# A three-layer kernel on one core: one written order for every loop step, the K split by DMA, and a fixed order where the second expert layer starts

## The chip, the cores and the metric

One core of one Trainium2 chip runs the whole program. The metric is the device time of an execution in microseconds (us). PE is TensorE, DVE is VectorE, ACT is ScalarE, POOL is GpSimd, SP is SyncE, which here only issues DMAs (its queue is SPq). Each engine works through its own queue in order; between engines the order is kept by semaphores.

## The reference

Three layers follow one another; the output is that of the third. All matrices are float32.

```
scores = (q @ k.T) / 8                        # 4 batches, 8 heads, 576 x 576, head size 64
kth    = 32nd largest score of the row
attn   = softmax(scores where scores >= kth)
x      = attn @ v                             # as 2304 tokens x 512
h      = x @ w_in                             # 512 x 2048
y      = (h * clip(h + 3, 0, 6) / 6) @ w_out  # 2048 x 512
logits = normed(y) @ normed(expert_emb).T / tau     # 8 experts
e, gate = argmax(logits), softmax(logits)[e]
out    = gate * (relu(y @ w1[e]) @ w2[e])     # 512 x 1024, 1024 x 512; each token by its own expert
```

## The kernel before, in words

Every float32 product is made of three faster ones: an operand is rounded to a high part (a cast on ACT), the low part is the difference (a subtraction on POOL or DVE), and high x high, high x low and low x high add up in PSUM.

**The loop.** The attention is cut into 72 units (128 rows of two heads, or a remainder of 64 rows of four). `step(i)` runs 76 times and issues, in one fixed order, pieces of five units in different stages: the scores of unit i (PE L368, copied by ACT L371, paired maxima on DVE L380 to L384), the 32 largest values of unit i-1 (`select`, DVE L399 and L402), the masking of unit i-2 (`relu` on ACT L416, `mask` on POOL L420), the exponent of unit i-3 (ACT L426) with its sum, reciprocal and scaling (POOL L430, DVE L433, POOL L442; ACT L440 for the first 16 units), and the transposes (PE L453, copies ACT L458) and the product with v (PE L471) of unit i-4. `manual_schedule` means that each engine's queue has the instructions in the order in which the program issues them.

**The second layer inside the loop.** Two 128-token groups that are done are pushed as eight items; from step 12 on each step takes one item (none in the steps named in `PAUSE`): `s1` (24 matmuls, PE L530), `gate`, `swish`, `large`, `small`, and, for the item of the step before, `s2` (2 x 6 matmuls, PE L563). The low parts of the weights come back from DRAM (`fetch`, 512 KB each, SP L251).

**The weights of the second layer** arrive as 64 pieces of 64-bit words. `convert_w` takes two pieces at a time: it first calls `load_w`, which issues loads as long as fewer than five pieces are waiting (buffers `stg`, five), then makes float32 of the words on DVE (L221, L223, L229), ACT (L226) and POOL (L227); `split_w` makes the high part (ACT L240), the low part (POOL L241) and stores that (SP L236). One pair per step in steps 0 to 7, then two.

**K.** `load_k` loads each head twice, into partitions 0 to 63 and 64 to 127, in two halves of 288 columns (SP L288, buffers `kraw`, five). `need_k` casts all (ACT L296) and the upper 64 partitions get the low part by a subtraction, one half on POOL (L349), the other on DVE (L352).

**Routing.** A finished group y goes through four side steps, one per loop step: `r1` (squares, transposes), `r2` (logits, DVE maximum and index, one-hot L609), `r4` (rank among the tokens of its expert by a triangular matmul, L615, L616, and the running count `acc` on POOL), `r5` (table row, DVE L626, L627, and a scatter into the table `tbl` by POOL L628).

**After the loop** no order is written; the tile scheduler sets it. The remaining items run back to back (`whole`). Once 16 groups are counted (`order`), `ahead` starts the third layer: the first expert's weights, the ids of its first 256 tokens, its gathers, the split of w1. After the last items the last two groups are routed; only then are all ids known. `stage1` is the first product of an expert (PE L917), `stage2` the second (PE L930), `split2` the split of w2 (ACT L734, DVE L735), `tokens` gathers tokens (POOL L750) and transposes them (PE L754), `load_ids` reads the table (SP L716).

Of the kernel before, what the change touches and what calls it, by code (L numbers as in the profile page):

```python
# [8 lines left out]
F32 = mybir.dt.float32  # L9
# [29 lines left out]
PAUSE = (13, 17, 31, 35, 49, 53, 66, 67)  # L39
HS = S // 2  # L40
# [4 lines left out]
SIDE = 100  # L45
# [38 lines left out]
def layers(tc: tile.TileContext, qt, kt, v, w_in, w_out, embt, tau, w1, w2, out, y_dram, g_dram, x_dram, tbl, lo_dram, flag, pools, consts):  # L84
# [13 lines left out]
    acc = const.tile([128, E], BF16, name="acc")  # L98
# [3 lines left out]
    viol = const.tile([128, NUNIT, 2, 2], BF16, name="viol")  # L102

# [32 lines left out]
    def embed(part):  # L136
# [6 lines left out]
        elif part == 1:  # L143
            onesf = mp.tile([128, 128], F32, tag="ug", name="onesf", bufs=4)
# [15 lines left out]
    def setup():  # L160
        nc.vector.memset(ones, 1.0)
        nc.vector.memset(acc, 0.0)
        nc.gpsimd.iota(iota8, pattern=[[1, 8]], base=0, channel_multiplier=0, allow_small_or_imprecise_dtypes=True)
        nc.gpsimd.iota(ebase, pattern=[[STRIDE, 8]], base=0, channel_multiplier=0, allow_small_or_imprecise_dtypes=True)
# [5 lines left out]
        padt = mp.tile([128, E * STRIDE * 2 // 128], I32, tag="ug", name="padt", bufs=4)  # L170
        nc.gpsimd.memset(padt, PAD)
        nc.sync.dma_start(out=tbl.rearrange("(p a) b -> p (a b)", p=128), in_=padt)
        zr = mp.tile([128, DM], F32, tag="ug", name="zr", bufs=4)
# [7 lines left out]
    wpieces = deque()  # L181
# [7 lines left out]
    wraw = deque()  # L189
    whole_w, small_w = deque(), deque()  # L190
    cnt = [0]

    def load_w():

        while wpieces and len(wraw) < 5:
            src, dst = wpieces.popleft()
            if src.dtype == F32:
# [5 lines left out]
            wraw.append((raw, dst, src.dtype == F32))  # L203

    def convert_w():


        load_w()
        words, two = [], [wraw.popleft() for _ in range(min(2, len(wraw)))]
        if not two:  # L210
            return
        both = mp.tile([128, DM], F32, tag="ug", name="wf", bufs=4)
        for o, (raw, dst, single) in enumerate(two):
            full = both[:, 256 * o:256 * o + 256]
            if single:
                nc.vector.tensor_copy(full, raw)
            else:
                cnt[0] += 1
                words.append((raw, full.bitcast(I32), cnt[0] % 4 != 3))
        for raw, t, _ in words:  # L220
            nc.vector.scalar_tensor_tensor(t, raw[:, :, 1], 3, raw[:, :, 1], op0=ALU.logical_shift_left, op1=ALU.bitwise_xor)  # L221
        for raw, t, _ in words:
            nc.vector.scalar_tensor_tensor(t, t, 0x3FFFFFFF, raw[:, :, 1], op0=ALU.bitwise_and, op1=ALU.bitwise_xor)  # L223
        for raw, t, rounded in words:
            if rounded:
                nc.scalar.activation(raw[:, :, 0], raw[:, :, 0].bitcast(U32), AF.Copy, scale=2.0 ** -29)  # L226
                nc.gpsimd.tensor_tensor(t, t, raw[:, :, 0], op=ALU.add)  # L227
            else:
                nc.vector.scalar_tensor_tensor(t, raw[:, :, 0], 29, t, op0=ALU.logical_shift_right, op1=ALU.bitwise_or)  # L229
        whole_w.append((both,) + two[0][1])  # L230

    def split_w():

        while small_w:
            lo, full = small_w.popleft()
            nc.sync.dma_start(out=lo, in_=full)  # L236
        while whole_w:
            full, hi, lo = whole_w.popleft()
            x = full if len(hi.shape) == 2 else full.rearrange("p (k n) -> p k n", k=2)
            nc.scalar.copy(hi, x)  # L240
            nc.gpsimd.tensor_tensor(x.bitcast(F32R), x, hi.bitcast(F32), op=ALU.subtract)  # L241
            small_w.append((lo, full))
# [4 lines left out]
    def fetch(n, m):  # L247

        if m < total and m not in lows_[n]:
            lows_[n][m] = t = lop.tile([128, 1024], F32R, tag=f"l{n}", name=f"lo{n}")  # L250
# [25 lines left out]
    low, low2 = deque(), deque()  # L276
# [3 lines left out]
    def load_k(i):  # L280
# [3 lines left out]
        for h in (2 * p, 2 * p + 1):  # L284
            if (b, h) not in K and (b, h) not in kraws:
# [4 lines left out]
    def need_k(b, h):  # L290
        if (b, h) in K:
            return
        t = kp.tile([128, S], F32R, tag="k", name="kst")
        for g, raw in enumerate(kraws.pop((b, h))):
            c = slice(HS * g, HS * g + HS)
            nc.scalar.copy(t[:, c], raw)  # L296
            (low if g else low2).append((t[64:128, c], raw[64:128, :], t[64:128, c].bitcast(F32)))
        K[b, h] = t
# [27 lines left out]
    def prep(i):  # L326
# [15 lines left out]
        if u[0] == "t":  # L342
            need_k(u[1], 2 * u[3])
            need_k(u[1], 2 * u[3] + 1)

    def lows():
# [3 lines left out]
        while low2:  # L350
            o, x, h = low2.popleft()
            nc.vector.tensor_tensor(o, x, h, op=ALU.subtract)  # L352
# [737 lines left out]
```

## Time and profile before

| | |
|---|---|
| time, median of 3 runs | 1183.14 us (1183.0 to 1194.14) |
| the profiled execution's own time | 1184.85 us |
| its span, first to last instruction | 1183.1 us |
| PE busy | 1026.0 us (87%), 7224 matmuls |
| DVE busy | 838.1 us (71%) |
| ACT busy | 732.1 us (62%) |
| POOL busy | 645.7 us (55%) |
| mean granted TensorE clock | 0.938 of 2.4 GHz |

An engine's busy time is that of its instructions, without its waits. The granted clock is given as a share of full speed: 1.00 is 2.4 GHz, 0.50 is 1.2 GHz, and a value between them is a stretch that had both. Matmuls overlap, so their single durations add up to more than the time they take.

### The profile page before, as it was taken

The page shows a single profiled execution, that of the slowest core. Times are in us where ns is not written, and L with a number is a line of the kernel's source. Part 1 is how long each engine was busy: PE and PEld are TensorE (multiplying, and loading weights), DVE is VectorE, ACT ScalarE, POOL GpSimd, SP SyncE. Part 2 cuts the span into 40 slices and gives each one's busy share as a digit, 9 for nine tenths or more (in the row PEclk, how much of TensorE's full clock was granted, in tenths as well). Part 3 has the DMA queues.
Part 4 walks back from the last instruction along what each step waited for, and adds up shares of the span by engine and source line. Part 5 has one row for each costly group of instructions (what it writes and reads, how often), then busy time and mean ns, then how long its engine had stood idle before and what let it go on. Part 6 is the DMA issues. An engine that isn't in the chain of part 4 may idle for free. (4 is left out here: it accounts for less than half of the span.)

```text
span 1183.1 us, 21477 instructions
## 1 busy us (share of the span) xinstructions
PE 1026.0 (87%) x7224; PEld 885.8 (75%) x7224; DVE 838.1 (71%) x2714; ACT 732.1 (62%) x1518; POOL 645.7 (55%) x846
## 2 busy tenths in 40 slices
PE   2476766699999899999899999999998898999994
PEld 1354555578888788888788878889987787888883
DVE  6999977998899998899998899611244343445440
ACT  5688768777777877777877787642334343444540
POOL 5667767686777786777786766623231433113200
PEclk9966778789999999999999998999998899999997
DMA  7335555655324445424454333346781564244540
GB/s 212 120 100 174 164 177 187 195 179 197 122 90 155 127 160 184 121 89 155 115 183 157 121 92 115 110 142 178 210 276 32 187 217 171 71 176 147 174 166 20
DMA packets 97113, 176.49 MB, mean 149 GB/s; under 512 B 21135, under 2 KB 46882, under 8 KB 96991
## 3 DMA queue, kind: packets, MB, share of 16 engines
q1 hardware_dynamic: 92351, 164.90, 43.4%
q0 software_dynamic: 4640, 10.10, 2.5%
q8 instruction: 60, 0.98, 0.3%
q14 instruction: 62, 0.51, 0.1%
HBM read 155.87 MB, written 19.71 MB: 148 GB/s over the span
## 5 line engine op out<-in xcount | busy, mean ns | idle before, releaser
L420 POOL TENSOR_TENSOR s<-s,z 128x576 f32<-128x576 f32 x144 | 186.0, 1292 | 13.0 <-ACT z L416 11.5
L530 PE MATMUL bank_h<-xh,vh 128*128 128x256 f32 x576 | 172.1, 299 | 2.7 <-ACT xh L488 1.6
L530 PE MATMUL bank_h<-xh,lo 128*128 128x256 f32 x576 | 166.7, 289 | 7.1 <-DMA lo<-lo_dram 7.1
L530 PE MATMUL bank_h<-xl,vh 128*128 128x256 f32 x576 | 166.2, 288 | 0.6 <-DVE xl L489 0.6
L399 DVE MAX8 A<-left 128x8 f32<-128x288 f32 (+1 forms) x288 | 160.0, 596 | 0.0
L453 PE MATMUL bank_t<-ident,s 128*128 128x128 f32 x648 | 110.2, 297 | 53.1 <-ACT s L440 26.1
L547 POOL TENSOR_TENSOR gl<-u,gh 128x512 fp32r<-128x512 f32 x72 | 93.2, 1294 | 79.0 <-ACT gh L544 78.0
L453 PEld LDWEIGHTS bank_t<-ident,s 128*128 128x128 f32 x648 | 76.1, 149 | 75.8 <-ACT pt L458 37.7
L368 PE MATMUL ps_sc<-kst,qh 128*128 128x288 f32 x256 | 88.8, 359 | 49.1 <-ACT s L371 24.1
L536 ACT ACTIVATE u<-bank_h,half 128x512 f32<-128x512 f32 x72 | 49.5, 687 | 118.9 <-PE bank_h L530 118.9
L563 PE MATMUL y<-wh,gh 128*128 128x512 f32 x288 | 120.0, 418 | 0.0
L530 PEld LDWEIGHTS bank_h<-xh,vh 128*128 128x128 f32 x576 | 113.3, 197 | 8.1 <-issue 3.1
L530 PEld LDWEIGHTS bank_h<-xh,lo 128*128 128x128 f32 x576 | 113.2, 196 | 8.3 <-DMA lo<-lo_dram 8.3
L563 PE MATMUL y<-lo,gh 128*128 128x512 f32 x288 | 115.9, 403 | 0.0
L530 PEld LDWEIGHTS bank_h<-xl,vh 128*128 128x128 f32 x576 | 113.4, 197 | 1.4 <-DVE xl L489 1.0
L735 DVE TENSOR_TENSOR l<-a,h 128x1024 fp32r<-128x1024 f32 x64 | 77.4, 1232 | 51.9 <-ACT h L734 45.7
L563 PE MATMUL y<-wh,gl 128*128 128x512 f32 x288 | 114.2, 401 | 0.0
L416 ACT ACTIVATE z<-s,zb 128x576 bf16<-128x576 f32 x144 | 112.7, 782 | 1.0 <-DVE zb L405 0.8
L426 ACT ACTIVATE s<-s,nb 128x576 f32<-128x576 f32 x144 | 111.7, 775 | 0.0
L458 ACT COPY pt<-bank_t 128x384 f32<-128x384 f32 x216 | 95.6, 479 | 24.4 <-PE bank_t L453 24.4
L540 DVE SCALAR_TENSOR_TENSOR u<-u,bank_h 128x512 f32<-128x512 f32 x72 | 49.2, 684 | 83.8 <-ACT u L536 83.7
L471 PE MATMUL bank_a<-pt,vt 128*64 128x128 f32 (+1 forms) x1600 | 105.4, 285 | 0.0
(230 smaller groups left out, 2819.9 us busy)
## 6 DMA issues: line engine op xcount, KB each, us to landing
lo<-lo_dram SPq DMA_DIRECT2D x144, 512.0 KB, 4.3
a<-in_moe_w_dram SPq DMA_DIRECT2D x64, 512.0 KB, 8.7
kraw<-in_k_dram SPq DMA_DIRECT2D x64, 144.0 KB, 2.6
qraw<-in_q_dram SPq DMA_DIRECT2D x64, 128.0 KB, 3.3
w<-in_moe_w_in_dram SPq DMA_DIRECT2D x32, 256.0 KB, 3.9
w<-in_moe_w_out_dram SPq DMA_DIRECT2D x32, 256.0 KB, 3.5
lo_dram<-wf SPq DMA_DIRECT2D x32, 256.0 KB, 2.1
vt<-in_v_dram SPq DMA_DIRECT2D x16, 320.0 KB, 4.1
```

The lines of the kernel that those rows point to most:

```text
L368: nc.tensor.matmul(ps[:, n, :HS], t, kk[:, HS * g:HS * g + HS], start=(o == 0), stop=(o == len(parts) - 1))
L399: nc.vector.max(A[:, n, 8 * r:8 * r + 8], src[:, n, :w])
L416: nc.scalar.activation(zb_[n], tile_of(i, n), AF.Relu, bias=sel[i][2][:, n:n + 1], scale=-BIG)
L420: nc.gpsimd.tensor_tensor(s, s, zb_[n], op=ALU.subtract)
L426: nc.scalar.activation(s, s, AF.Exp, bias=sel[i][1][:, n:n + 1], scale=SCALE, accum_out=sums[i][:, n:n + 1])
L453: nc.tensor.transpose(pp[:, 128 * k:128 * k + 128], e[:, 128 * (3 * c + k):128 * (3 * c + k) + 128], ident)
L458: nc.scalar.copy(pts[i][:, 3 * c:3 * c + 3, :].rearrange("p k n -> p (k n)"), tb_.pop((i, c))[:, :384])
L471: nc.tensor.matmul(av[64 * n:64 * n + 64, c0:c1], vt[:, k, 64 * n:64 * n + 64], pt[:, k + 5 * n if k < 4 else 4, c0:c1], start=(o == 0), s ...
L530: nc.tensor.matmul(ph[:, a, :], w, x[:, k, :], start=(k == 0 and n == 0), stop=(k == 3 and n == 2))
L547: nc.gpsimd.tensor_tensor(state[q][1], state.pop((q, "u")).rearrange("p (a n) -> p a n", a=2), state[q][0].bitcast(F32), op=ALU.subtract)
L563: nc.tensor.matmul(state["y"][o], x[:, a, c], w, start=(f == 0 and n == 0), stop=(f == 15 and n == 2))
L735: nc.vector.tensor_tensor(lo, x, hi.bitcast(F32), op=ALU.subtract)
```

## The change

**The loop step** becomes a table of names: `FIRST` for steps 0 to 20, `THEN` for the others. Each name is one piece of work as before; a few are cut finer (`s1` into its two halves, the weight conversion into `load`, `one`, `two`, `round`, `add`, `hi`, `low`, `store`). Weights are loaded one step ahead of their conversion (`load` has offset -1), one pair per step in steps 0 to 4 and two from step 5 on, and split and stored one step after it.

**K** is loaded once, two heads in one tile of 128 partitions; ACT casts it into both heads' tiles, POOL subtracts in place over all 128 partitions, and two DMAs (`ship`) carry the low halves into the other 64 partitions. DVE has no part in it.

**The threshold** of the mask (DVE L405, two per unit) moves into the POOL instruction that scales the maximum (`bounds`).

**Routing** of groups 0 to 11 is done four groups at a time: `choose` (one-hot picks and running counts), `rank` (table rows), and `place`, one scatter per step.

**The last two groups** are routed in a written order together with the first products of the first expert (two of their eight blocks, `stage1(0, 0, 256, (o,))`, stand between the transposes) and with the split of its second weights; the second expert's first weights (`load1(1)`) are loaded ahead of all that. The side steps after the loop get priority 600 instead of 100.

```diff
+RAMP, WORDS = 5, 21
+FIRST = ("turn0 lows ship hi0 expo0 low0 hi1 s10 keep0 load_k expo1 turn1 bend0 one0 guard pick0 store0 score0 low1 two0 mask0 pick1 "
+         "turn2 inverse s11 pick2 round1 bend1 keep1 take0 keep2 load_q mask1 s20 score1 round0 gate one1 scale two1 values swish "
+         "take1 large aside add0 store1 pick3 pairs load0 add1 xh load1 s21 small bounds xl prep need_v")
+THEN = ("pick0 turn0 turn1 expo0 keep0 s10 expo1 lows ship turn2 pick1 pick2 s11 keep1 keep2 guard bend0 score0 gate take0 load_k "
+        "values mask0 score1 inverse swish scale pick3 bend1 xh load_q take1 prep need_v mask1 bounds aside large s20 xl pairs "
+        "s21 small place")
...
-SIDE = 100
+SIDE = 600
...
+    def pair_of(i, c):
+        n = (i if c == 0 else -1) if i < RAMP else 2 * i - RAMP + c
+        return n if 0 <= n < 32 else -1
...
-                kraws[b, h] = [lp.tile([128, HS], F32, tag="kraw", name="kraw", bufs=5) for _ in range(2)]
-                for g in range(2):
-                    nc.sync.dma_start(out=kraws[b, h][g], in_=kt[b * H + h][:, HS * g:HS * g + HS])
+            kraws[b, p] = raw = lp.tile([128, S], F32, tag="kraw", name="kraw", bufs=2)
+            for n in range(2):
+                nc.sync.dma_start(out=raw[64 * n:64 * n + 64, :], in_=kt[b * H + 2 * p + n][64 * n:64 * n + 64, :])
...
+        nc.scalar.copy(k0, raw)
+        nc.scalar.copy(k1, raw)
+        low.append((raw.bitcast(F32R), raw, k0.bitcast(F32)))
+        ships.append((k0[64:128, :].bitcast(F32), raw[0:64, :]))
+        ships.append((k1[0:64, :].bitcast(F32), raw[64:128, :]))
...
-            for n in range(2):
-                nc.vector.tensor_scalar(zb[:, n:n + 1], A[:, n, TOPK - 1:TOPK], BIG, None, op0=ALU.mult)
...
-        nc.gpsimd.tensor_scalar(nb, A[:, :, 0], -SCALE, None, op0=ALU.mult)
+        nc.gpsimd.tensor_tensor(nb, A[:, :, 0:TOPK:TOPK - 1], kb, op=ALU.mult)
...
-            state[q, "u"] = u = mp.tile([128, DM], F32, tag="ug", name="u", bufs=4)[:, :2 * nt]
+            state[q, "u"] = u = mp.tile([128, DM], F32, tag="wf" if stored[0] == 32 else "ug", name="u", bufs=3 if stored[0] == 32 else 1)[:, :2 * nt]
...
-        side.extend((r1, r2, r4, r5))
+        side.extend((r1, r2))
+        if g % 4 == 3 and g < 12:
+            side.extend((choose, rank))
...
+        for name, f, j in (("load", w_load, -1), ("one", w_one, 0), ("two", w_two, 0), ("round", w_round, 0), ("add", w_add, 0),
+                           ("hi", w_hi, 1), ("low", w_low, 1), ("store", w_store, 1)):
...
+        for name in (FIRST if i < WORDS else THEN).split():
+            ops[name]()
...
+        with tc.manual_schedule():
+            for o in range(2):
+                last[6](last[0], o)
...
+            load1(1)
+            yts = []
+            for o, (t, g) in enumerate(finals):
+                pp = pps()
+                for k in range(4):
+                    nc.tensor.transpose(pp[:, k, :], t[:, 128 * k:128 * k + 128], ident)
+                yts.append(gp.tile([128, 4, 128], F32, tag="ob", name="ytl"))
+                nc.scalar.copy(yts[o], pp)
+                stage1(0, 0, 256, (o,))
...
+            choose()
...
+            stage1(0, 0, 256, (2, 3))
+            rank()
+            stage1(0, 0, 256, (4,))
+            split2(0, range(5, 8), lambda f: stage1(0, 0, 256, (f,)))
         with tc.high_priority(offset=500):
-            stage1(0, 0, 256)
-        split2(0)
+            while spots:
+                place()
```

## Rows read from the trace of the kernel before

**Rows 1.** One line of the program, L384, over the whole trace.

```profile
L384 DVE TENSOR_TENSOR left<-ps_sc,left x72: 445/445/450, 16.6 to 750.8; 128x288 f32<-128x288 f32 x72
```

**Rows 2.** Stretches: length, busy PE, PEld, DVE, ACT, POOL (instructions), granted clock, DMA share, GB/s.

```profile
0.00:17.00 17.00, 2.99 (x8) 1.98 (x8) 5.99 (x14) 9.84 (x22) 9.64 (x18) 1.00 0.78 231
17.00:55.60 38.60, 15.90 (x66) 12.01 (x67) 38.31 (x132) 23.01 (x49) 24.20 (x34) 1.00 0.46 137
55.60:128.70 73.10, 49.82 (x273) 38.16 (x273) 72.78 (x254) 61.55 (x134) 52.34 (x69) 0.63 0.45 143
128.70:258.70 130.00, 92.28 (x629) 78.41 (x630) 110.09 (x353) 93.60 (x206) 90.47 (x112) 0.80 0.57 182
258.70:751.30 492.60, 472.23 (x3833) 410.08 (x3831) 454.32 (x1648) 376.20 (x831) 355.55 (x500) 0.99 0.43 136
751.30:886.00 134.70, 130.05 (x903) 116.09 (x903) 37.53 (x117) 50.94 (x96) 44.86 (x49) 1.00 0.62 187
886.00:931.60 45.60, 35.80 (x199) 30.18 (x199) 15.35 (x63) 15.68 (x28) 7.52 (x9) 0.85 0.40 128
```

**Rows 3.** Waits, 128.7 to 258.7 us: who waited for whom, us, times, longest.

```profile
PE bank_t L453 <- ACT s L440: 13.1, 4, 5.2
...
ACT w L226 <- DMA w<-in_moe_w_in_dram: 12.1, 3, 5.4
...
ACT w L226 <- DMA w<-in_moe_w_out_dram: 9.4, 3, 4.0
```

**Rows 4.** Groups of DVE instructions, 128.7 to 258.7 us.

```profile
L221 DVE SCALAR_TENSOR_TENSOR wf<-w 128x256 int32<-128x256 int32 x32 | 14.5, 483 | 4.1 <-DMA w<-in_moe_w_in_dram 3.4 <-DMA w<-in_moe_w_out_dram 0.7
L223 DVE SCALAR_TENSOR_TENSOR wf<-wf,w 128x256 int32<-128x256 int32 x32 | 12.6, 435 | 0.0
...
L352 DVE TENSOR_TENSOR kst<-kraw,kst 64x288 fp32r<-64x288 f32 x8 | 7.0, 918 | 0.1
...
L405 DVE TENSOR_SCALAR zb<-A 128x1 f32<-128x1 f32 x18 | 2.4, 145 | 0.0
```

**Rows 5.** The page's DMA issues: one group.

```profile
kraw<-in_k_dram SPq DMA_DIRECT2D x64, 144.0 KB, 2.6
```

**Rows 6.** SP's queue in order of time, 385 to 400 us.

```profile
388.34 9.39 SPq L288 DMA_DIRECT2D kraw<-in_k_dram  x4
397.84 0.38 SPq L251 DMA_DIRECT2D lo<-lo_dram  x1
```

**Rows 7.** DVE in order of time, 401 to 406 us and 802 to 803 us.

```profile
402.69 1.36 DVE L609 TENSOR_SCALAR oh<-iota,ixf 128x8 bf16<-128x8 f32 x1
404.08 1.94 DVE L352 TENSOR_TENSOR kst<-kraw,kst 64x288 fp32r<-64x288 f32 x2
...
802.72 0.23 DVE L609 TENSOR_SCALAR oh<-iota,ixf 128x8 bf16<-128x8 f32 x1
```

**Rows 8.** Groups of DVE instructions, 258.7 to 751.3 us.

```profile
L352 DVE TENSOR_TENSOR kst<-kraw,kst 64x288 fp32r<-64x288 f32 x16 | 10.4, 691 | 0.2
L626 DVE SCALAR_TENSOR_TENSOR po<-po,oh 128x8 f32<-128x8 f32 x11 | 10.2, 927 | 0.0
...
L609 DVE TENSOR_SCALAR oh<-iota,ixf 128x8 bf16<-128x8 f32 x11 | 7.3, 665 | 0.4
```

**Rows 9.** PE in order of time, 754 to 756 us.

```profile
755.67 0.55 PE L453 MATMUL bank_t<-ident,s 128*128 128x128 f32 x3 [0.49 <-ACT pt L458]
```

**Rows 10.** PE and POOL in order of time, 905 to 932 us.

```profile
909.14 0.17 PE L615 MATMUL bank_t<-oh,tri 128*128 128x8 bf16 x1 [4.37 <-DVE oh L609]
...
925.80 0.90 PE L754 MATMUL pxt<-ident,xg 96*128 96x96 f32 x4 [3.38 <-DMA xg<-y_dram,idt]
...
917.39 0.98 POOL L750 DMA_INDIRECT xg<-y_dram,idt  x1 [6.09 <-DMA idt<-tbl]
...
931.63 0.38 PE L917 MATMUL ph<-xh__10794,h 128*128 128x224 f32 x2
```

**Rows 11.** The page's groups of instructions: the costliest of POOL.

```profile
L420 POOL TENSOR_TENSOR s<-s,z 128x576 f32<-128x576 f32 x144 | 186.0, 1292 | 13.0 <-ACT z L416 11.5
```

More of the change, by code (lines that the diff above doesn't have):

```diff
@@ L202, in load_w @@
                 nc.sync.dma_start(out=raw, in_=src.bitcast(I32).rearrange("p (n two) -> p n two", two=2))
[L203 to L214, printed above, removed]
-            if single:
[L216 to L220, printed above, removed]
+                cnt[0] += 1
@@ L230, in convert_w, with parts_of @@
[L230 to L242, printed above, removed]
+    def parts_of(e):
+        hi, full = e["dst"][0], e["both"]
+        return hi, full if len(hi.shape) == 2 else full.rearrange("p (k n) -> p k n", k=2)
@@ L274, in tile_of @@
         return sbuf[i % NS][:, n, :]
-    low, low2 = deque(), deque()
+    low, ships = deque(), deque()
     kraws = {}
@@ L636, in whole, with place @@
+    def place():
+        if not spots:
+            return
+        g = spots.popleft()
+        w_ = nc.gpsimd.indirect_dma_start(out=tbl, out_offset=bass.IndirectOffsetOnAxis(ap=rows[:, g:g + 1], axis=0),
+                                          in_=ids[:, g, :], in_offset=None)
+        if not looping[0]:
+            tc.declare_no_dep(w_.ins, group="places", reason="every token has one place")
+            tc.add_to_no_dep_group("places", w_.ins)
     def whole(item, last):
@@ L648, in whole, with part @@
         return item
-    def part(item, k):
+    def part(item, k, *half):
         if item:
-            item[k](item[0])
+            item[k](item[0], *half)
     late = {}
@@ L665, in order @@
         pc = half_a()
[L666 removed]
+        nc.tensor.matmul(pc[:, :E], ones, before[:, NG - 2, :], start=True, stop=True)
         cnt = fs.tile([1, E], F32, tag="cnt", name="cnt")
@@ L772, in ahead @@
         load2(0)
+        expert(1)
     def step(i, last):
+        a = moe.popleft() if moe and i not in PAUSE else None
         def at_(j, f, *a):
@@ L779, in at_ @@
                 f(i - j, *a)
-        more = iter(range(1 if i < 8 else 2))
-        def words():
-            if next(more, None) is not None:
-                convert_w()
-        a = moe.popleft() if moe and i not in PAUSE else None
-        at_(2, relu, 0)
-        at_(2, mask, 0)
-        at_(3, expo, 0)
-        lows()
-        split_w()
-        load_k(i + 2)
-        at_(1, select, 0)
-        at_(1, select, 1)
-        part(a, 1)
-        part(a, 2)
-        part(a, 3)
-        words()
@@ L800, in step @@
-        for c in range(2):
-            at_(4, turned, c)
-            at_(4, keep, c)
-        at_(0, scores, 0)
-        at_(4, turned, 2)
-        at_(4, keep, 2)
-        at_(0, take, 0)
-        at_(1, select, 2)
-        words()
-        at_(3, expo, 1)
-        at_(3, guard)
-        if last:
-            last[6](last[0], 0)
-        part(a, 4)
-        part(a, 5)
-        at_(0, scores, 1)
-        at_(0, take, 1)
-        at_(1, select, 3)
-        at_(3, inverse)
-        if i - 3 >= EARLY:
-            at_(3, scale)
@@ L821, in step @@
-        at_(2, relu, 1)
-        at_(2, mask, 1)
-        at_(1, bounds)
-        if last:
-            last[6](last[0], 1)
-        split_w()
-        at_(0, pairs)
-        words()
-        load_q(i + 3)
-        if i + 1 < NU and units[i + 1][0] == "r":
-            prep(i + 1)
-        if i + 2 < NU and (units[i + 1][0] != "r" or units[i + 2][0] != "r"):
-            prep(i + 2)
-        if i - 3 < EARLY:
-            at_(3, scale)
-        at_(4, values)
-        at_(4, finish)
-        need_v(i)
@@ L839, in step, with aside, after, preps @@
-        if side:
-            side.popleft()()
+        def aside():
+            if side:
+                side.popleft()()
+        def after(o):
+            if last:
+                last[6](last[0], o)
+        def preps():
+            if i + 1 < NU and units[i + 1][0] == "r":
+                prep(i + 1)
+            if i + 2 < NU and (units[i + 1][0] != "r" or units[i + 2][0] != "r"):
+                prep(i + 2)
+        ops = dict(load_k=lambda: load_k(i + 2), load_q=lambda: load_q(i + 3), need_v=lambda: need_v(i), lows=lows, ship=ship, prep=preps,
+                   s10=lambda: part(a, 1, 0), s11=lambda: part(a, 1, 1), gate=lambda: part(a, 2), swish=lambda: part(a, 3), large=lambda: part(a, 4), small=lambda: part(a, 5),
+                   s20=lambda: after(0), s21=lambda: after(1), aside=aside, place=place,
+                   guard=lambda: at_(3, guard), inverse=lambda: at_(3, inverse), scale=lambda: at_(3, scale), bounds=lambda: at_(1, bounds),
+                   pairs=lambda: at_(0, pairs), values=lambda: at_(4, values), xh=lambda: at_(4, finish), xl=lambda: at_(4, finish_low))
```

301 lines of the change are left out of this document (192 added, 109 removed).

## The prediction

> **What bounds the kernel now.** The page's list of engines comes first, and it misleads: PE is busy 87% of the span, but that is a mean over stages with different limits. The page's chain of waits helps little either: it follows the last scatters and says nothing of the 1100 us before them. So the span is cut into stages. The last instruction of the paired maxima, L384, marks the end of a loop step, 72 times [rows 1]; the stretches of the table of busy times end at such marks: after steps 0, 4, 11, 20 and 71 [rows 2]. The reader is to compare in each line the length with the busiest engine.
>
> Steps 1 to 11 (38.6 and 73.1 us) are DVE's: 111.1 of 111.7 us busy. Steps 12 to 20 take 130.0 us, 14.4 a step, and belong to nobody: DVE 110.1, ACT 93.6, PE 92.3, POOL 90.5, and PE has a mean granted clock of 0.80, a mix of 2.4 and 1.2 GHz. There the table of waits is read: ACT stands 21.5 us in all in front of weight words that have not landed, and PE 13.1 us in front of a scaling on ACT that is queued behind them [rows 3]. Steps 21 to 71 take 492.6 us, 9.66 a step, and are PE's: 472.2 busy at a clock of 0.99, with DVE close behind (454.3). The rest of the second layer (134.7 us) is PE's almost wholly. In the handover to the experts (45.6 us) PE works 35.8 us and the clock is 0.85. The expert stage behind it is left as it is, and I take no change there.
>
> **Steps 0 to 11.** Removed from DVE: L352 for the first units, and L405 twice a unit. Rows 4 price them at 0.92 us beside POOL's work and 0.145 us: with some four L352 and 22 L405 about 2.9 to 3.7 and 3.2 us. Added: the weights go to two pairs per step at step 5 instead of 8, so three pairs more fall here. A pair costs 2 x 0.483 + 2 x 0.435 = 1.84 us on DVE [rows 4], together 5.5. Since DVE bounds this stretch, the sum counts, and it is near 0. In step 0 the low half of K has one leg more, a `ship` DMA of 144 KB. No DMA inside SBUF is in the trace; the nearest row is the load of K of the same size, 2.6 us [rows 5]. So 0 to +2.6 us; I take 1, since the first scores end long before step 0 does (17.0 us for 6.0 of DVE). Later ships have most of a step: K of unit i+2 is cast in step i, shipped in i+1, used in i+2.
>
> **Steps 12 to 20.** DVE loses the same three pairs (5.5), eight L352 (7.0) and 18 L405 (2.4) [rows 4]: 110.1 - 14.9 = 95.2 us. ACT and POOL lose their part of the three pairs and stay below that. What is left to decide is the 19.9 us for which DVE stood still. The new table loads weights in the step before (`load`, four DMAs, behind `add` of the same step), makes the high and low parts one step later, and gives each step's ACT and POOL work inputs from the step before. `load` waits on SP for POOL's `add`, since there are still five buffers; behind it on SP stand the second load, the fetch of `s21` and `need_v`, none of which is wanted before the middle of the next step, while the first words are wanted at its start: `one0` is DVE's first instruction. So I leave half of the standstill, 10 us: 105 us, a gain of **25**. Ends: 95.2 (a gain of 35) and no gain, 130, if the loads are still late.
>
> **Steps 21 to 71.** DVE loses 16 L352 (10.4), 102 L405 (14.8 at 0.145) and of routing 11 L626 (10.2) and 11 L609 (7.3) [rows 4, 8]; `choose` and `rank`, three batches of some ten small instructions, add 5 to 10. That matters only where DVE, not PE, ends the step: in the steps without an item and in those with new K. One of these shows what is mended: a small one-hot instruction took 1.36 us beside POOL and 0.23 us alone, the two L352 behind it 1.94 us [rows 7]. SP also stood for 9.39 us on four K loads, whose buffers were not free, with a low-weight load queued behind them [rows 6]; the new K has two loads and two ships per pair of heads, as many issues as before, but two buffers of whole pairs. PE's idle time here is 492.6 - 472.2 = 20.4 us, the most that can be won without removing PE work, and almost none is removed. I take half, a gain of **10**. The other end is a new wait: the nearest row is the wait of the third transposes for the copy of the first, 0.49 us where no scores stand between [rows 9]; in all 51 steps that is 25 us lost. The table puts half of `s1` between them, so I take the gain. POOL's `bounds` is one instruction as before, and `relu` now waits for it rather than for DVE; it stands a step ahead.
>
> **The second layer's rest** is full of PE work already: 0, with 3 us to either side for the new priority.
>
> **The handover.** Before, PE waited 4.37 us for the one-hot of group 17, and the ids of the first expert's other tokens were read 6.09 us late for POOL, so PE waited another 3.38 us for their gather; only at 931.6 us did `stage1` go on [rows 10]. Lost are 45.6 - 35.8 = 9.8 us of idle time [rows 2]; and a clock of 0.85 means 30% of the stretch, 13.7 us, at 1.2 GHz, which cost some 3 us if PE was busy in half of it. The written order has two blocks of `stage1` behind the transposes and two more behind the logits, so that one-hot, ranks and scatter go on beside them; routing's chain should be some 8 us shorter, and the gather's wait mostly gone. Behind the scatters stand, on POOL, only the gathers, which need them. I take a gain of **9**; ends: 13, or a loss of 2 if the fixed order makes PE wait for the copies.
>
> **The sum.** 1 - 25 - 10 + 0 - 9 = -43 us against the profiled execution's own 1184.85 us: 1141.9. The median of the runs is 1.7 us below that execution, so 1140.
>
> A rule weighed here: the Trainium skill, page "SBUF — State Buffer", section "SBUF: two separate sides", says that DVE with two SBUF inputs and POOL hold one port pair exclusively, so that the later one stands still for the other's whole instruction. The trace agrees in L352 and disagrees on its limits: L609, with one tensor input, went from 0.23 to 1.36 us too [rows 7].
>
> **Rivals.**
>
> *The steady steps get a new wait on PE, slower.* The transposes are now at the head of PE's step and need POOL's scaling of the step before, which stands behind a mask, which stands behind `relu`, which now waits for POOL's `bounds`. If POOL slips by one mask, 1.29 us [rows 11], and PE waits for it in each of 51 steps, that is +66 us in place of the -10: 1184.85 + 1 - 25 + 66 - 9 - 1.7 = 1216. It decides from (1 - 25 - 9) / 51, about 0.65 us a step. For it: many links through three engines in one fixed order. Against it: POOL is busy only 355.6 of 492.6 us [rows 2]. 0.13, with the next one.
>
> *DVE is blocked by POOL.* The weight words are eight two-input instructions per step of two pairs. If POOL, now denser, blocked each by half of its 1.29 us, 13 such steps would lose 8 x 0.65 x 13 = 67 us, which gives 1207. This is what the skill's rule just named would do at its worst. Against it: L221 is at 0.483 us in rows 4 with POOL busy 70% of the time, hardly more than L223 (0.435). 0.03 of the 0.13.
>
> *The weights stay late.* Steps 12 to 20 keep their waits and give nothing but the removed DVE work where it counts, say 4 us: 1161. For it: same buffers, and `load` still behind `add`. 0.16.
>
> *The steady steps give nothing, or lose the 0.1 to 0.3 us each that eats up 5 to 15 us.* 1150 to 1165. 0.12.
>
> *Gains and losses cancel.* The change does not do what it says: the ramp gains 10, the steady steps lose 0.3 us each (15), the handover gives 2: about 1187. 0.09.
>
> **How the numbers follow.** The forecast, 1120 to 1150, has 0.45; better than 1120 0.05. With both late-weights (0.16) and no-gain (0.12) that makes 0.78 for faster by over 1% (below 1171, about what a measurement of this kernel tells from no change); 0.09 within 1%; 0.13 slower. All gains at their ends are 35 + 20 + 13 + 2 = 70: 1113. The range goes from 1113 to 1180: it holds forecast, late weights and no gain, and half of the cancelled case; outside are the slower rivals and about 0.06.
>
> **What would show it.** Steps 12 to 20 between two L384 marks: 105 us is right, over 125 refutes the ramp; ACT's waits for weight words should be below 8 us. Steps 21 to 71: 483 us, with PE idle below 12; a line of waits of the transposes for POOL's scaling above 30 us would be the slower rival. L352 and L405 are gone from DVE. In the handover PE's waits for the one-hot and the gather fall below 3 us in all and the clock is above 0.95. Wrong would be above all a PE that stands still at the head of each step.

## The result, and the profile after

The changed kernel takes 1166.68 us (median of four runs, 1164.9 to 1169.58) beside 1183.07 of the kernel before on the same chip: a ratio of 0.984, with an interval of 0.980 to 0.988. It is faster by 1.6%, 16 us, where 43 us were forecast. The table puts the two profiled executions side by side, cut at the same marks; the mark's line is now L413.

| stretch | before, us | after, us | forecast | measured |
|---|---|---|---|---|
| steps 0 to 11 | 128.7 | 146.4 | +1 | +17.7 |
| steps 12 to 20 | 130.0 | 115.9 | -25 | -14.1 |
| steps 21 to 71 | 492.6 | 488.2 | -10 | -4.4 |
| from there to the experts' first 224-column block | 180.3 | 168.3 | -9 | -12.1 |
| from there to the end | 251.5 | 244.4 | 0 | -7.0 |
| span | 1183.1 | 1163.2 | -43 | -19.9 |

Busy times by stretch, the columns of [rows 2]:

```profile
0.00:18.00 18.00, 2.85 (x8) 1.99 (x8) 3.79 (x11) 8.03 (x15) 7.90 (x17) 1.00 0.65 183
18.00:58.90 40.90, 16.49 (x67) 12.69 (x67) 40.41 (x122) 25.64 (x53) 27.16 (x33) 1.00 0.50 151
58.90:146.40 87.50, 49.93 (x274) 40.08 (x274) 87.26 (x253) 63.90 (x141) 63.05 (x77) 0.60 0.45 146
146.40:262.30 115.90, 87.08 (x623) 76.93 (x624) 111.33 (x313) 88.00 (x186) 86.63 (x105) 0.81 0.59 183
262.30:750.50 488.20, 466.88 (x3837) 420.45 (x3836) 418.52 (x1456) 379.86 (x819) 346.05 (x487) 0.98 0.45 137
750.50:886.00 135.50, 130.37 (x895) 116.98 (x894) 39.52 (x90) 50.81 (x92) 47.18 (x49) 1.00 0.65 193
886.00:918.75 32.75, 29.01 (x185) 25.30 (x183) 16.23 (x54) 16.73 (x28) 6.67 (x8) 0.95 0.58 176
```

In steps 5 to 11 (58.9 to 146.4) VectorE (DVE) has one instruction fewer than before (253 against 254) and is busy 14.5 us longer; it fills the stretch, as before. The count hides an exchange: 13 weight-word products more (some 5.4 us) for 14 L405 fewer (1.9 us), which makes 3.5 us. The other 11 us mean that instructions have become longer. Which ones, the groups of the same steps say (busy time, mean ns of one), first before, then after:

```profile
L221 DVE SCALAR_TENSOR_TENSOR wf<-w 128x256 int32<-128x256 int32 x22 | 11.4, 559 | 0.0
L223 DVE SCALAR_TENSOR_TENSOR wf<-wf,w 128x256 int32<-128x256 int32 x22 | 8.2, 413 | 0.0
...
L229 DVE SCALAR_TENSOR_TENSOR wf<-w,wf 128x256 int32<-128x256 int32 x6 | 2.5, 411 | 0.0
```

```profile
L238 DVE SCALAR_TENSOR_TENSOR wf<-wf,w 128x256 int32<-128x256 int32 x28 | 18.9, 712 | 0.0
L234 DVE SCALAR_TENSOR_TENSOR wf<-w 128x256 int32<-128x256 int32 x28 | 10.5, 413 | 0.0
...
L241 DVE SCALAR_TENSOR_TENSOR wf<-w,wf 128x256 int32<-128x256 int32 x7 | 9.4, 1340 | 0.0
```

L234, L238 and L241 are L221, L223 and L229 of the kernel before. L238 took 0.413 us there and takes 0.712 now, in one shape; L241 went from 0.411 to 1.340. L234 was the longer one before (0.559) and is now at 0.413. The order of time shows what stands beside them, first DVE, then POOL, in one step (start, duration):

```profile
97.50 1.94 DVE L238 SCALAR_TENSOR_TENSOR wf<-wf,w 128x256 int32<-128x256 int32 x2
99.36 1.50 DVE L241 SCALAR_TENSOR_TENSOR wf<-w,wf 128x256 int32<-128x256 int32 x1
100.79 0.51 DVE L428 MAX8 A<-top 128x8 f32<-128x144 f32 x2
```

```profile
96.42 1.33 POOL L263 TENSOR_TENSOR wf<-wf,wh 128x512 fp32r<-128x512 f32 x1
97.70 2.88 POOL L446 TENSOR_TENSOR s<-s,z 128x576 f32<-128x576 f32 x2
100.54 0.93 POOL L251 TENSOR_TENSOR wf<-wf,w 128x256 int32<-128x256 int32 x1
```

The three word products need 1.94 + 1.50 us where three alone need some 1.2, and each ends some 0.3 us after one POOL instruction ends and the next begins (97.70, between the two masks, and 100.54). In the steady steps a second loss is seen, in the four steps that bring a new K pair (37, 38, 55 and 56: 11.64, 13.46, 12.22, 13.16 us beside 9.1 to 9.9 of their neighbours). SP's queue and ScalarE (ACT) in step 38:

```profile
416.68 1.13 SPq L331 DMA_DIRECT2D kst<-kraw  x2
417.86 0.58 SPq L279 DMA_DIRECT2D lo<-lo_dram  x1
418.50 1.13 SPq L315 DMA_DIRECT2D kraw<-in_k_dram  x2
```

```profile
424.38 0.67 ACT L322 CAST kst<-kraw 128x576 fp32r<-128x576 f32 x1 [3.51 <-DMA kraw<-in_k_dram]
426.81 0.46 ACT L484 COPY pt<-bank_t 128x384 f32<-128x384 f32 x1
```

The load is issued at 418.5, behind `ship`, in the very step whose `prep` copies the data; ACT stands 3.51 us for it, and the transposes' copies (L484) and with them PE stand behind it. PE's wait for these copies in steps 21 to 71 was 2.7 us before; after, it is

```profile
PE bank_t L479 <- ACT pt L484: 14.5, 11, 2.9
```

### The profile page after: what moved, and what is told of

It reads as the page before. It is cut to its first block, busy times and chain, and to the rows that moved or that the text cites. A ratio compares the mean times of both kernels' runs of the same rounds, so it can differ in the third digit from the quotient of the medians.

```text
span 1163.2 us, 21146 instructions
## 1 busy us (share of the span) xinstructions
PE 1008.5 (87%) x7200; PEld 892.1 (77%) x7200; DVE 818.5 (70%) x2429; ACT 732.6 (63%) x1486; POOL 646.4 (56%) x833
## 5 line engine op out<-in xcount | busy, mean ns | idle before, releaser
L446 POOL TENSOR_TENSOR s<-s,z 128x576 f32<-128x576 f32 x144 | 189.8, 1323 | 70.2 <-ACT z L442 69.5
L568 PE MATMUL bank_h<-xh,vh 128*128 128x256 f32 x576 | 177.0, 307 | 0.8 <-DVE u L580 0.8
L484 ACT COPY pt<-bank_t 128x384 f32<-128x384 f32 x216 | 100.4, 475 | 59.1 <-PE bank_t L479 58.9
L479 PE MATMUL bank_t<-ident,s 128*128 128x128 f32 x648 | 108.2, 294 | 28.0 <-ACT pt L484 16.7
L397 PEld LDWEIGHTS ps_sc<-kst,qh 128*128 128x128 f32 x256 | 55.7, 218 | 88.4 <-issue 73.6
L400 ACT COPY s<-ps_sc 128x576 f32<-128x576 f32 x144 | 91.5, 635 | 41.8 <-PE ps_sc L397 38.4
L603 PE MATMUL y<-wh,gh 128*128 128x512 f32 x288 | 116.3, 404 | 0.0
L479 PEld LDWEIGHTS bank_t<-ident,s 128*128 128x128 f32 x648 | 82.3, 150 | 44.0 <-ACT pt L484 20.1
L442 ACT ACTIVATE z<-s,nb 128x576 bf16<-128x576 f32 x144 | 111.7, 780 | 0.8 <-POOL nb L436 0.7
```

The source lines that it names most:

```text
L397: nc.tensor.matmul(ps[:, n, :HS], t, kk[:, HS * g:HS * g + HS], start=(o == 0), stop=(o == len(parts) - 1))
L400: nc.scalar.copy(sbuf[i % NS][:, :, HS * g:HS * g + HS], ps_[i][:, :, :HS])
L442: nc.scalar.activation(zb_[n], tile_of(i, n), AF.Relu, bias=sel[i][1][:, n, 1:2], scale=-BIG)
L446: nc.gpsimd.tensor_tensor(s, s, zb_[n], op=ALU.subtract)
L479: nc.tensor.transpose(pp[:, 128 * k:128 * k + 128], e[:, 128 * (3 * c + k):128 * (3 * c + k) + 128], ident)
L484: nc.scalar.copy(pts[i][:, 3 * c:3 * c + 3, :].rearrange("p k n -> p (k n)"), tb_.pop((i, c))[:, :384])
```

## The experiments

They ran on three chips, where the kernel before took 1186.8 us (e1 to e4), 1191.1 (e5 to e8) and 1190.0 (the others). All but e6, c1 and c2 are one execution each. So each is read by its stretches, between the same marks, and e6, c1 and c2 also by their ratios to the kernel before on the same chip. Stretches that an edit leaves alone show the noise: steps 21 to 71 took 487.9 to 489.8 us in the six variants that have them as in the changed kernel, but what stands behind step 71 took 412 to 423 us in the six that leave it and the steady order as changed.

### The ramp

**One name moved.**

```
- ... store0 score0 low1 two0 mask0 pick1 turn2 inverse s11 pick2 ... round0 gate one1 scale two1 ...
+ ... store0 score0 low1 mask0 pick1 turn2 inverse s11 pick2 ... round0 gate two0 one1 scale two1 ...
```

> The changed kernel with one name moved in the ramp's written list: two0 (VectorE's second word products of the step's first pair) stands behind pick2, ahead of one1, and no longer between low1 and mask0. Marks as in the changed kernel's profile: steps 0-11 took 146.4 us, steps 12-20 115.9, steps 6-11 12.66 us each. Theory A, the order: a two-input word product on VectorE stands still for as long as POOL works on a long instruction beside it, and only two0 was written beside the masks; then VectorE's own 10.4 us bound the step: steps 6-11 10.4 to 11.0 each, steps 0-11 133 to 137, steps 12-20 108 to 113, the time about 1148 to 1155. Rival B, exclusion wherever they are written: POOL's 9.2 us and the words' 9 x 0.41 = 3.7 us of a step add up to 12.9, whatever the order: steps 6-11 12.3 to 12.8, the time 1163 to 1168. Rival C, the pace (three pairs more in steps 0-11) costs it: no change either, and the word products' mean durations stay at 0.71 and 1.34 us only under B.

Measured: 1146.24 us, 20 less than the changed kernel on its chip. Steps 0 to 11 took 132.8 us, steps 12 to 20 108.2, step 6 11.31 and steps 7 to 11 10.92 each. That is Theory A; steps 0 to 11 and the time came out at or a little under its ranges. The same groups of DVE in steps 5 to 11:

```profile
L234 DVE SCALAR_TENSOR_TENSOR wf<-w 128x256 int32<-128x256 int32 x28 | 14.2, 547 | 0.0
L238 DVE SCALAR_TENSOR_TENSOR wf<-wf,w 128x256 int32<-128x256 int32 x28 | 10.5, 416 | 0.0
...
L241 DVE SCALAR_TENSOR_TENSOR wf<-w,wf 128x256 int32<-128x256 int32 x7 | 2.9, 418 | 0.0
```

L238 and L241 are back at 0.42 us, 14.9 us less; L234 is 3.7 us more. The sum, 11.2, is the whole of what this stretch became shorter by (87.5 to 76.3 us). Where L234's part comes from, one step shows, DVE and then POOL:

```profile
104.40 0.75 DVE L238 SCALAR_TENSOR_TENSOR wf<-wf,w 128x256 int32<-128x256 int32 x2
105.07 0.42 DVE L241 SCALAR_TENSOR_TENSOR wf<-w,wf 128x256 int32<-128x256 int32 x1
105.41 1.29 DVE L234 SCALAR_TENSOR_TENSOR wf<-w 128x256 int32<-128x256 int32 x2
106.62 0.75 DVE L238 SCALAR_TENSOR_TENSOR wf<-wf,w 128x256 int32<-128x256 int32 x2
```

```profile
102.00 2.52 POOL L446 TENSOR_TENSOR s<-s,z 128x576 f32<-128x576 f32 x2
105.28 0.79 POOL L251 TENSOR_TENSOR wf<-wf,w 128x256 int32<-128x256 int32 x1 [0.77 <-ACT s L400]
```

The two masks now run beside DVE's maxima, which read one tensor and are not slowed (two of 288 columns take 0.80 us at 102.84 beside a mask, and 0.80 us at 101.84 in the changed kernel with POOL idle), and take 2.52 us in place of 2.88; `one1` (L234) falls beside `add0` (L251).

**The pace.** `RAMP` 7 in place of 5: two of the three pairs that steps 0 to 11 gained go back behind them.

```
- RAMP, WORDS = 5, 21
+ RAMP, WORDS = 7, 21
```

> The changed kernel with two weight pairs a step from step 7 on and not from step 5: 17 pairs begun by the end of step 11, where the changed kernel has 19 and the kernel before 16. Theory A (the pace is a small part of the 17.6 us that steps 0-11 lost, the order the larger): steps 5 and 6 fall from 11.6 and 12.7 to 9.2-10, steps 0-11 from 146.4 to 140-142, and steps 18 and 19 take them back: steps 12-20 from 115.9 to 119-122; steps 7-11 stay at 12.66; the time 1164-1169. Rival B, the pace is the cause: steps 7-11 fall too (10.5-11.5), steps 0-11 under 137.

Measured: 1168.13 us; steps 0 to 11 142.4, steps 12 to 20 120.9; steps 5, 6 and 7 fell to 10.25, 9.90 and 11.60, steps 8 to 11 stayed at 12.65 to 12.68. Theory A, with steps 5 and 7 and the sum of steps 0 to 11 a little outside what it says. Steps 5 to 7 became 5.1 us shorter, and steps 12 to 20 5.0 longer; steps 0 to 4, which the edit leaves alone, happened to take 1.1 more. So two of the three pairs are worth some 5 us, and the place of `two0` 13.6 of the 17.7 us lost in steps 0 to 11; each was measured with the other left as it was, so they need not add up.

**Words further apart**, tried together with the K repair below.

```
- ... gate one1 scale two1 values ... pick3 pairs load0 ...
+ ... gate one1 two0 scale values ... pick3 two1 pairs load0 ...      (two0 gone from its old place)
```

> As e6_two0_and_k, with the ramp's four lots of word products spread: one1 stands ahead of two0 and two1 behind pick3. In e1_two0_after_pick2 the 28 products of one0 and one1 in steps 5-11 still took 0.547 us on the mean beside 0.413, as POOL's add0 runs right behind two0 and so beside one1. Theory A (a word product stands still beside POOL's two-input work, by the order): with a one-input maximum (1.41 us) beside add0 the mean falls to 0.41-0.45 and steps 6-11 from 10.92 to 10.3-10.6 us, about 6 us over the ramp's thirteen full steps: 1120-1126. Rival B: the pair's later end delays ScalarE's rounding and POOL's adds of the next step: no gain or a loss of up to 8: 1127-1137.

Measured: 1143.49 us, steps 6 to 11 at 11.4, steps 12 to 20 at 115.0 (109.6 without the spreading, in e6 below, on the same chip). Theory A of this run missed, and Rival B's loss came: the products of `one0` and `one1` rose to 0.630 us on the mean. `two1` and POOL's adds end later, so that POOL's next `low0` slides under `one0`:

```profile
89.90 1.78 DVE L234 SCALAR_TENSOR_TENSOR wf<-w 128x256 int32<-128x256 int32 x2
```

```profile
89.78 1.28 POOL L263 TENSOR_TENSOR wf<-wf,vh 128x512 fp32r<-128x512 f32 x1
```

It is the same collision at another place of the step; a list is judged only by the order in time that comes out of it.

### K

```
- load_k=lambda: load_k(i + 2)
+ load_k=lambda: load_k(i + 3)        (and load_k(2) ahead of the loop)
```

> The changed kernel with each K pair's load issued one step earlier (step i loads for unit i+3, not i+2; still two raw buffers). In the changed kernel the four steps 37, 38, 55, 56 took 11.64, 13.46, 12.22 and 13.16 us beside 9.1 to 9.9 of their neighbours, and ScalarE's K copies waited 3.5 us for the transfer. Theory A: the load is issued in the step that copies it and lands 4.3 us later, behind the ship transfers: the four steps fall to 9.2-10.2, steps 21-71 from 488.2 to 474-477, the time to 1152-1155. Rival B: the wait comes from ScalarE's and POOL's own queues (two K copies and a 1.3 us subtraction more in these steps), not from the transfer: steps 21-71 stay at 486-489. Rival C: SP stands behind the ship's end with the new load and hands the second layer's tables on late: steps 21-71 490 or more.

Measured: 1154.76 us; steps 21 to 71 471.6, steps 37, 38, 55 and 56 at 7.95, 9.20, 7.95 and 8.79. Theory A, and 16.6 us where 11 to 14 were expected. Steps 0 and 1 lost 6.9 us, which was not expected: ahead of the loop the third load stands on SP behind a `ship` at 10.88 us, and the next loads of q and of weight words come at 12.06 and 12.68 us, where the changed kernel has them at 9.01 and 9.63.

### The written order of the steady steps

The list `THEN` written in the order of the kernel before; the second of the three has K early from step 4 on, and `ship load_k` behind `swish`; the third has also the two threshold products on DVE again.

```
- THEN = "pick0 turn0 turn1 expo0 keep0 s10 expo1 lows ship turn2 ... bend0 score0 ... load_k ... mask0 ..."
+ THEN = "bend0 mask0 expo0 lows ship load_k pick0 pick1 s10 s11 gate swish turn0 keep0 turn1 keep1 score0 ..."
```

> The changed kernel with the steady steps (21-71) written in the order of the kernel before; the K scheme, the removed VectorE instructions, the ramp and the hand-over stay as changed. Steps 21-71 took 492.6 us before and 488.2 changed, of which about 14 us stand in four steps with a late K. Theory A: the new order carries the gain of the steady steps and the K scheme takes it away: 498-507 us. Rival B: the order is worth nothing, the removed VectorE work is: 486-490. Rival C: the new order itself made K late (its load stands 21st in the list, behind the ship, while in the old order it stands at the head): the four steps at 9.5-10.5 and the whole under 486.

Measured: 1219.44 us, steps 21 to 71 531.9: worse than any of the three theories had it.

> The changed kernel with the steady steps in the order of the kernel before, as in e3_steady_order_before (531.9 us for steps 21-71), but with K loaded a step earlier from step 4 on, and ship and the K load behind the second layer's first products, so that SP hands its tables on first. Theory A: e3's 44 us beside the changed kernel were SP's queue (tables standing behind ship, 14.5 us of TensorE's waits) and K: steps 21-71 476-492. Rival B: the order of TensorE's, ScalarE's and POOL's own instructions is worth it: 500-520. The new order with K early took 471.6; the difference to it is the order's own worth.

Measured: 1199.14 us, steps 21 to 71 509.2, Rival B's range; 22.7 us of e3's loss were K and the tables queued on SP. PE's wait for the tables in steps 21 to 71, e3 and then e8:

```profile
PE bank_h L568 <- DMA lo<-lo_dram: 14.5, 4, 4.9
```

```profile
PE bank_h L568 <- DMA lo<-lo_dram: 4.1, 2, 2.4
```

But 509.2 is also 16.6 more than the kernel before needed in the same order. ACT's waits name a suspect:

```profile
ACT z L442 <- POOL nb L436: 69.2, 47, 2.1
```

> As e8_old_order_k_early (steps 21-71 in the old order, K a step early: 509.2 us, where the kernel before took 492.6 in the same order), with the two thresholds of the mask computed on VectorE again, as before, right behind the last maximum, and no longer by POOL's product behind the masks. In e8 ScalarE waited 69.2 us in 47 steps for that product at the head of the list. Theory A: that wait is the whole of e8's loss against the kernel before: steps 21-71 488-495. Rival B: something else of the change slows the old order (the split halves of the second layer's products, the routing pieces, the K scheme's POOL work): 503-510, with the wait gone.

Measured: 1181.17 us, steps 21 to 71 492.1: Theory A, and within 0.5 us of the kernel before's 492.6. So what else the change does in these steps, 27 us less work on DVE among it (427.3 us busy after 454.3), is worth next to nothing in the old order. The change's parts in the steady steps are: thresholds on POOL, 17 us dearer in the old order; the new order, with thresholds on POOL and K early, 471.6, which is 20.5 us better than 492.1; and K late, which takes 16.6 of them back. The new order with the thresholds on DVE was not run, so what the order is worth by itself is not shown.

### Behind the loop

**The hand-over left to the scheduler.**

```
-        with tc.manual_schedule():
+        with tc.high_priority(offset=500):
             for o in range(2):
                 last[6](last[0], o)
```

> The changed kernel with the hand-over (the two last token groups' logits, choice, ranks, and the first expert's first products) left to the scheduler at a priority of 500 instructions ahead, as before's first expert was, in place of the written order. From step 71's end to the first 224-column block 180.35 us before, 168.25 changed; the clock of the stretch 870-960 rose to over .95. Theory A: the written order (first products beside the routing) carries the 12 us: 175-181. Rival B: the shorter routing chain (one choice for two groups, one rank matmul pair) carries it: 166-171. The expert stage from the first 224-column block on: 203.9 us under both.

Measured: 1178.7 us; step 71's end to the 224-column block 175.5 us, Theory A at its lower end (168.4 and 170.2 in e2 and e1 on the same chip, which leave the hand-over alone). Against these the written order is worth 5 to 7 us, and PE's waits for token gathers in this stretch are 9.1 us (7.8 and 1.3), where e1 has 4.7 and e2 2.4; the second expert's weights are still loaded early there (893.7 us). e3, on the same chip, leaves the hand-over alone as well and took 175.9, but with more of PE's work behind its last mark (165.4 us busy, against 161.2 in e1 and 161.3 in e4). The stage behind the block took 248.5, against 243.9 and 244.3.

**The second expert's first weights late.**

```
-            load1(1)                          (ahead of the routing)
-                if r:
-                    load1(then)
+                load1(then)                   (in the loop over the experts, as before)
```

> The changed kernel with the second expert's first weights loaded where the kernel before loads them, in the loop over the experts, and no longer at the hand-over's head. From the first 224-column block (918.75 us) to the last block the changed kernel took 203.9 us, before 209.5; with what follows 244.5 and 251.5. Theory A, the early weights: the experts' stage gained its 7 us because the second expert's products no longer stand behind its weights: 249-252 us from the block on, the time about 1171-1174. Rival B, the token gathers (TensorE's 11.0 us of waits on them before are 1.9 us after, as the written hand-over places the tokens earlier): 243.5-246, the time 1164-1168. A quieter queue at the hand-over (up to 3 us sooner to the 224-column block) is possible under both.

The 11.0 us in this expectation count waits ahead of the block too; from the block on they are 6.5 before and 1.9 after.

Measured: 1184.23 us, 254.6 us from the block on. That speaks for Theory A, but the three other variants on that chip, which leave this alone, took 248.4, 248.8 and 250.6, all above the changed kernel's 244.4. So it stands once more beside the changed kernel itself, on one chip:

> The changed kernel itself, on the chip of this call, as the measure for c2_load1_late_again: behind step 71 it took 412.7 us in its first profile, while three variants that leave that part as it is took 418 to 426 on another chip at a lower granted clock. Expected: steps 0-71 within 3 us of 750.5 on any chip; behind them 410-427.

> The same kernel as e5_load1_late (the second expert's first weights loaded in the loop over the experts), beside c1_changed_again on one chip, since e5's 430.5 us behind step 71 stood beside 418.4 to 426.0 of other variants on its chip. Theory A, the early weights carry the experts' 7 us: c2 is 4-8 us slower than c1, behind the first 224-column block. Rival B, they carry nothing: within 2 us.

Measured: c1 1171.87 us (0.9825 of before, 0.979 to 0.986), steps 0 to 71 752.2 and 417.9 us behind them; c2 1184.81 us (0.9936, 0.991 to 0.997). By the medians the early weights are worth 12.9 us, more than Theory A said, and every run of c2 is slower than every one of c1. The profiled executions differ by more, 18.4 us behind step 71 (c2's is its slowest run): 6.3 us ahead of the block (168.8 us from step 71's end against 175.1), 12.1 behind it. SP's queue, c1 and then c2:

```profile
889.20 1.93 SPq L793 DMA_DIRECT2D a<-in_moe_w_dram  x4
905.88 4.72 SPq L788 DMA_DIRECT2D idt<-tbl  x8
912.06 2.20 SPq L802 DMA_DIRECT2D a<-in_moe_w_dram  x4
```

```profile
908.04 4.37 SPq L788 DMA_DIRECT2D idt<-tbl  x8
912.80 2.15 SPq L793 DMA_DIRECT2D a<-in_moe_w_dram  x4
916.40 2.51 SPq L802 DMA_DIRECT2D a<-in_moe_w_dram  x4
```

Early, the weights (L793) move while the routing runs and no gather is out. Late, they are issued together with the next ones (L802), right when the first expert's token gathers start (POOL issues them at 910.0 us and later in c1, at 911.5 and later in c2), and PE waits for these, c1 and then c2 from step 71 on:

```profile
PE pxt L826 <- DMA xg<-y_dram,idt: 4.1, 4, 1.1
```

```profile
PE pxt L826 <- DMA xg<-y_dram,idt: 12.3, 5, 5.0
PE po L977 <- ACT hh L966: 6.0, 2, 5.6
```

So Theory A's cause, the place of the load, works in good part through the wait that Rival B named, that for the gathers. What held ACT before the 5.6 us the trace does not name.

### Both repairs together

`two0` behind `pick2`, and K early from step 4 on (`load_k=lambda: (load_k(i + 2), load_k(i + 3) if i > 3 else None)`), everything else as changed.

> The changed kernel with both repairs: two0 behind pick2 (which alone took steps 0-11 from 146.4 to 132.8 us and steps 12-20 from 115.9 to 108.2) and, from step 4 on, each K pair's load a step earlier (which alone took steps 21-71 from 488.2 to 471.6, and lost 6.9 us in steps 0 and 1, which this form leaves alone). If the two are independent: 132.8 + 108.2 + 472 and 168 and 244.5 behind it, a span of 1126 and a time of 1126-1131 us, 0.950 to 0.955 of the kernel before. Rival: what the ramp gave is taken back behind it (the second layer's rest or the hand-over waits for something that does not depend on the ramp): 1135-1148.

Measured: 1140.12 us (1139.46 to 1141.12), 0.957 of the kernel before (0.951 to 0.964), and so faster than both kernels (the changed one has 0.980 to 0.988 on its chip). Its stretches: steps 0 to 11, 12 to 20, 21 to 71, to the block, the rest:

```profile
0.00:133.10 133.10, 65.66 (x349) 52.77 (x349) 117.76 (x383) 97.27 (x207) 95.34 (x126) 0.82 0.56 167
133.10:242.70 109.60, 82.93 (x623) 74.02 (x623) 101.22 (x314) 87.98 (x186) 84.43 (x105) 0.86 0.64 193
242.70:716.80 474.10, 459.46 (x3838) 413.56 (x3836) 418.23 (x1457) 379.65 (x819) 346.70 (x486) 1.00 0.47 141
716.80:888.75 171.95, 163.35 (x1076) 145.53 (x1076) 56.46 (x146) 67.49 (x120) 53.95 (x58) 0.96 0.64 186
888.75:1139.30 250.55, 229.37 (x1321) 200.38 (x1319) 100.13 (x135) 99.30 (x157) 61.54 (x60) 0.96 0.38 136
```

The time is 9 us above the expected range and in the rival's. The loop adds up nearly as expected: 716.8 us against 132.8 + 108.2 + 472. Behind it 422.5 us stand against 412.5 expected; e7 and e8 on the same chip took 418.4 and 426.0 there, so the 10 us may be that chip's (the clock in these two stretches is 0.96, where the changed kernel had 0.99 and 0.98). e1, which has the ramp's repair alone, took 414.5 us behind the loop on another chip and took nothing back; so the rival is unlikely, but here it is not excluded.

## Why the prediction was half right

**Steps 0 to 11: the failed step.** It says: "Since DVE bounds this stretch, the sum counts, and it is near 0." That DVE's instructions add up to the time was right. The pairs were sized low: e10 gives two of them some 5 us where 1.84 each was taken. The 1 us for step 0 is what was measured (18.0 us after 17.0), though no run shows that it is the `ship`. Wrong above all was that each instruction kept the duration of [rows 4]. In the table, `two0` stands between `low1` and `mask0`, POOL's two longest kinds of instruction; e1 moved that one name and took 13.6 us away; 4.1 of the 17.7 us are left. The rival "DVE is blocked by POOL" named the mechanism and got 0.03, because L221 stood at 0.483 us with POOL busy 70% of the time. That mean, over steps 12 to 20, hid the single collisions. The trace of before has them: in steps 5 to 11 L221 stood at 0.559 us beside L223's 0.413, and at 96.67 us two of L221 took 1.55 us beside POOL's L420 and L349. A mean of another list told nothing of a list that puts the two side by side. The rival's price, half of POOL's 1.29 us for each of eight instructions in 13 steps, was too high: three of nine products in a step were held, for 2.3 us (1.94 + 1.50 less 0.75 and 0.41), and e1 won 21.3 us in the whole ramp (13.6 + 7.7).

The rule of the Trainium skill weighed there, page "SBUF — State Buffer", section "SBUF: two separate sides", has the later of two such instructions stand for the whole of the other. The runs agree, word products of 0.42 us taking up to 1.5. DVE instructions with one tensor from SBUF were not held where the runs show them: the maxima beside the masks took their 0.80 us for two, and L411, which reads one of its two from PSUM, took 0.745 to 0.749 us in all 72 steps of the changed kernel. L609 of [rows 7], with one tensor, is no disagreement with the rule's limits, as the prediction has it: the same section names a second case, a DVE instruction in a two-port mode, and whether L609 was one no run here shows. The prediction cited the rule with the right direction and gave it too little weight.

**Steps 12 to 20.** "So I leave half of the standstill, 10 us: 105 us" was right in its wait: DVE stands still 4.6 us (115.9 - 111.3), and ACT's waits for weight words, 21.5 us in [rows 3], are gone from the list of waits, whose smallest entry is 0.3; POOL now waits 6.8 us for such words (0.4 before). No run takes the earlier loads back alone, so that they did it is argued. The other term failed: DVE was to fall to 95.2 us and is at 111.3, with the same collision in it. In e1 the stretch takes 108.2 us, DVE 101.6.

**Steps 21 to 71.** "I take half, a gain of 10" came out at 4.4 as the difference of two terms that were not in the sum: 21.0 from the order with the rest of the change (492.6 to 471.6 in e2) and 16.6 lost to K. That a small gain was left is luck. For K the text counted issues, "as many issues as before, but two buffers of whole pairs", and priced nothing; the load stands behind `ship` in the step that needs it, and this was to be read in the list (`ship` before `load_k` before `prep`). The limit of 20.4 us of PE idle time was no limit: PE's busy time itself fell, from 472.2 us before to 459.2 in e2, at 3833 and 3837 matmul records and a clock of 0.99 and 1.00. In the old order of e9 it stayed at 469.7, so it goes with the order; by what, no run here tells apart. The slower rival, PE at the head of each step behind POOL's scaling, did not come: PE's wait for it was 0.2 us. Its premise, ACT waiting for POOL's `bounds`, is true of the old order (69.2 us in e8); in the changed kernel ACT's waits have no line of it, and `bend0` is the 17th name there and not the first.

**The hand-over and the experts.** "I take a gain of 9" against 12.1. In the last part, up to the block, PE's wait for the one-hot (4.4 us) is gone, that for the gathers fell from 4.5 to 2.7, and the clock rose from 0.85 to 0.95: mechanism right, size a little low. From step 71's end on PE was idle 14.5 us before and 8.9 after; the rest of the 12.1 is busy time (165.9 and 159.4 us), of which clock and fewer matmuls (1102 and 1078 records) are not told apart. "I take no change there", for the expert stage, was wrong by 7: `load1(1)`, moved in the diff from the experts' loop to the hand-over, was taken as part of the routing's rearrangement and never costed. It carries 12.9 us (c1 and c2) and the written order 5 to 7 (e4), where 19.1 were gained behind step 71; no run takes both back.

**The time.** 1166.68 us lies in the range of 1113 to 1180, but not by the cases that the text put there for it: ACT's waits for words are gone, and the steady steps brought a gain and a loss of their own. What cost most, DVE standing for POOL, is the rival that it had put outside, at 1207.

## What to carry to other kernels

Before an order is written out by hand, put the two-tensor instructions of DVE and of POOL side by side in time: the price of one is not its duration in the old trace but what POOL runs at that moment. Look for it as a mean duration that grows in one shape of instruction, stage by stage; a mean over other steps hid it here. A load moved in a list has to be followed to its consumer, in steps and through SP's queue, and here its best place was a stretch in which no transfer was waited for (c1 and c2).

## What was not expected of the hardware

- Time in which a DVE instruction stands for POOL is shown as busy, not as a wait: DVE was 87.26 of 87.5 us busy with 14.9 us in it that e1 takes away from L238 and L241, and no table of waits has a line for it.
- It goes both ways: two of POOL's masks took 2.88 us beside word products and 2.52 beside maxima.
- Two `ship` transfers inside SBUF, 64 rows of 576 words each, took 1.13 us of SP to issue, as long as two loads of K from memory.
- The same instructions behind step 71 took 412.7 us on one chip and 417.9 on another (c1), more than the loop differed (750.5 and 752.2).
